# Softmax reciprocals by GpSimd partition broadcasts, projected keys transposed by the DMA crossbar, in six of eight batches

## Chip, cores, metric

One core of one Trainium2 chip (trn2). The metric is the device time of one execution in microseconds (us), median of several; lower is better. In the views PE is TensorE (PEld its weight loads), DVE is VectorE, ACT is ScalarE, POOL is GpSimd and SP is SyncE; POOLq and SPq are the DMA queues of the last two.

## The reference

Linformer attention, then a gated feed-forward stage. Per batch (8) and head (8), keys and values of 1024 positions are projected to 64 rows, then softmax over 64 columns:

```python
k_proj = np.einsum('ks,bhsd->bhkd', E, k)
v_proj = np.einsum('ks,bhsd->bhkd', F, v)
scores = (q @ k_proj^T) / sqrt(64); attn = softmax(scores)
attn_out = attn @ v_proj
x = attn_out as [8192, 512]
out = (sigmoid(x @ w_gate) * (x @ w_val)) @ w_out     # 512 -> 1536 -> 512
```

## The kernel before

Instructions are recorded in program order with what they read and write; semaphores follow from that. Each engine works through its own list in order. A "unit" is the feed-forward stage of batch b; the attention of batch b+1 is cut into ten pieces and put between its matmuls:

```python
def turn_k(ring):                      # keys transposed on TensorE
    bk = ring.next(); ob = bank[bk][:, :].bitcast(BF16)
    for r in range(NR):
        for g in range(2):
            mm(bk, ob[64*g:64*g+64, r*P:(r+1)*P], kp[:, r, :], ident[:, :], ..., tr=True, tp=(0, 64*g))
    act(kpD[...], ob[:, 0:512], [], ["kpD"], b=bk)

def den():      # ... column sums by matmul, then four reciprocals [128 x 128] into rden
def split():    # rhi = bf16(rden); rhl = both bf16 parts, for an exact-enough broadcast by matmul
def bc(rnd):    # spread the reciprocals over partitions by matmul
    for j in range(4):
        n, bk, jj = 4*rnd + j, att.next(), slice(32*j, 32*j + 32)
        mm(bk, bank[bk][:, :], bsel[jj, rnd, :, :]..., rhl[jj, :], ["bsel", "rhl"], tp=(32*j, 0))
        act(rb[:, n, :], bank[bk][:, :], [], [("rb", n)], b=bk)
def xo(r2):     # attn @ v_proj, then xT = that * rb  (VectorE; the "scaling" below)
...
return [kv, lambda: turn_k(att), lambda: sc(0), lambda: sc(1), den, split,
        lambda: bc(0), lambda: bc(1), lambda: xo(0), lambda: xo(1)]
```

`start_loads` mixes loads with iotas, from which VectorE makes the identity matrix:

```python
load_k(0)
pool(lambda e: e.iota(col_i[:, :], [[1, P]], channel_multiplier=0), w=["col_i"])
pool(lambda e: e.iota(row_i[:, :], [[1, 1]], channel_multiplier=1), w=["row_i"])
load_q_half(0, 0)
load_v(0)
# ... three more iotas, then the weights
```

The softmax here doesn't subtract the row's maximum and nothing guards it: scores larger than these inputs give would overflow.

## Time and profile before

| | us |
|---|---|
| median (lowest to highest of 4) | 581.01 (580.69 to 581.57) |
| span of the profiled run | 579.7 |
| TensorE (PE) busy | 559.1 |
| length of a repeated unit, six of them | 68.75 |

The prediction below shows the lines for these.

### The profile page before, as it was taken

The numbers are of one execution on the slowest core, as the hardware profiler recorded it, in microseconds if no ns is written. First come the engines' busy times: TensorE is split into PE (matmuls) and PEld (weight loads), VectorE is DVE, ScalarE is ACT, GpSimd is POOL, SyncE is SP. The second block draws the span as 40 slices with busy tenths as digits, with TensorE's granted clock in tenths as the row PEclk, the third lists the DMA queues.
The fourth block names the chain that finished last, engine by engine and source line by source line (L and its number), as shares of the span: only waits on it lengthen the run. The fifth ranks groups of instructions, "written<-read, shape, count | busy, mean of one in ns | idle before, by whom it ended". The sixth has DMA issues, their size and how long they took to land.

```text
span 579.7 us, 7813 instructions
## 1 busy us (share of the span) xinstructions
PE 559.1 (96%) x3150; PEld 253.9 (44%) x3206; DVE 253.3 (44%) x393; ACT 201.0 (35%) x371; POOL 30.3 (5%) x43
## 2 busy tenths in 40 slices
PE   5799899999999999999999999999999999999997
PEld 4444334444454444444444444444445444444443
DVE  2355265345633636236442365434463363633332
ACT  1454541444233351343323433243423335222220
POOL 8100010100100000000100001000000000000000
PEclk9999999999999999999999999999999999999999
DMA  9999998963943049511586027650411001000012
GB/s 153 201 206 193 139 165 155 183 133 75 162 97 75 31 109 181 91 38 48 101 162 110 19 73 117 139 92 36 74 54 38 35 21 37 37 36 20 36 37 90
DMA packets 70756, 55.04 MB, mean 95 GB/s; under 512 B 31168, under 2 KB 62400, under 8 KB 70720
## 3 DMA queue, kind: packets, MB, share of 16 engines
q0 software_dynamic: 31776, 29.89, 33.5%
q1 hardware_dynamic: 38944, 24.65, 16.5%
q8 instruction: 25, 0.41, 0.3%
q14 instruction: 11, 0.09, 0.1%
HBM read 60.29 MB, written 16.78 MB: 133 GB/s over the span
## 4 chain that ended last, share of the span: by engine, by line
PE 85%; DMA 10%; POOL 2%; DVE 1%; issue 1%; SPq 0%; POOLq 0%; DVEq 0%
PE pF L216 77%; PE pA L216 8%; DMA Qb<-in_q_dram 5%; DMA qT<-Qb 5%; DVE rden L685 1%; POOL wV L234 1%; POOL wG L234 1%; POOL KV L234 0%; POOL Qb L234 0%; SPq L622 0%; DVE rhl L695 0%; DVE ost L826 0%; DVE hT L799 0%; DVE rhi L693 0%; POOL pat_i L298 0%
## 5 line engine op out<-in xcount | busy, mean ns | idle before, releaser
L799 DVE SCALAR_TENSOR_TENSOR hT<-sig,pF 128x512 bf16<-128x512 f32 x192 | 131.2, 686 | 210.0 <-PE pF L216 140.0
L220 ACT ACTIVATE sig<-pF 128x512 f32<-128x512 f32 x192 | 115.3, 601 | 273.6 <-PE pF L216 266.1
L216 PE MATMUL pF<-xT,wG 128*128 128x512 bf16 x749 | 195.4, 380 | 2.2 <-issue 1.4
L216 PE MATMUL pF<-xT,wV 128*128 128x512 bf16 x748 | 195.1, 379 | 1.9 <-DVE xT L604 0.9
L216 PE MATMUL pF<-wO,hT 128*128 128x512 bf16 x704 | 163.4, 379 | 1.6 <-issue 1.1
L216 PEld LDWEIGHTS pF<-xT,wV 128*128 128x128 bf16 x768 | 75.1, 98 | 90.8 <-issue 0.6
L216 PEld LDWEIGHTS pF<-xT,wG 128*128 128x128 bf16 x768 | 71.2, 98 | 94.0 <-issue 14.5
L216 PEld LDWEIGHTS pF<-wO,hT 128*128 128x128 bf16 x720 | 68.7, 98 | 86.4 <-issue 5.8
L826 DVE TENSOR_SCALAR ost<-pF 128x512 f32<-128x512 f32 x60 | 41.5, 691 | 89.1 <-PE pF L216 89.1
L220 ACT ACTIVATE rb<-pA 128x512 f32<-128x512 f32 x62 | 32.2, 606 | 26.6 <-PE pA L216 26.6
L220 ACT ACTIVATE eT<-pA 128x512 bf16<-128x512 f32 x63 | 32.8, 603 | 11.3 <-PE pA L216 11.3
L733 DVE TENSOR_TENSOR xT<-pA,rb 128x512 bf16<-128x512 f32 x56 | 34.6, 680 | 0.0
L685 DVE RECIPROCAL rden<-pA 128x128 f32<-128x128 f32 x28 | 23.7, 908 | 0.0
L234 POOL DMA_DIRECT2D KV<-in_k_dram x8 | 7.2, 904 | 265.7 <-PE pF L216 208.6
L216 PE MATMUL pA<-KV,EFT 128*64 128x256 bf16 x240 | 14.6, 274 | 0.9 <-DMA KV<-in_k_dram 0.9
L220 ACT ACTIVATE kp<-pA 128x256 bf16<-128x256 f32 x8 | 3.1, 383 | 35.9 <-PE pA L216 35.9
L216 PEld LDWEIGHTS pA<-KV,EFT 128*64 128x64 bf16 x240 | 12.5, 110 | 4.1 <-issue 3.0
L216 PE MATMUL pA<-qT,kpD 64*64 64x512 bf16 (+1 forms) x140 | 10.6, 367 | 2.1 <-DMA qT<-Qb 1.8
L234 POOL DMA_DIRECT2D KV<-in_v_dram x8 | 7.1, 885 | 80.2 <-PE pA L216 80.2
L220 ACT ACTIVATE vpD<-pA 64x256 bf16<-64x256 f32 x28 | 10.5, 375 | 0.5
L216 PE MATMUL pA<-wO,hT 128*128 128x512 bf16 x47 | 10.5, 379 | 0.1
L216 PE MATMUL pA<-eT,vpD 64*64 64x512 bf16 (+1 forms) x136 | 10.4, 370 | 0.0
(72 smaller groups left out, 113.1 us busy)
## 6 DMA issues: line engine op xcount, KB each, us to landing
out_dram<-ost SPq DMA_DIRECT2D x64, 256.0 KB, 2.0
KV<-in_k_dram POOLq DMA_DIRECT2D x8, 1024.0 KB, 10.1
KV<-in_v_dram POOLq DMA_DIRECT2D x8, 1024.0 KB, 13.2
Qb<-in_q_dram POOLq DMA_DIRECT2D x7, 1024.0 KB, 15.0
wO<-in_moe_w_out_dram POOLq DMA_DIRECT2D x1, 1536.0 KB, 50.2
Qb<-in_q_dram POOLq DMA_DIRECT2D x2, 512.0 KB, 16.5
wG<-in_moe_w_gate_dram POOLq DMA_DIRECT2D x2, 512.0 KB, 23.8
wV<-in_moe_w_val_dram POOLq DMA_DIRECT2D x2, 512.0 KB, 25.6
```

Source lines behind the costliest of these rows:

```text
L216: return add("PE", lambda e: e.matmul(o, lhsT, rhs, **kw), r=r, x=[("bank", b)])
L220: return add("ACT", lambda e: e.activation(o, i, func, scale=scale), r=r, w=w, x=x)
L234: add("POOL", lambda e: e.dma_start(o, i), r=r, w=w, dma=sem)
L685: lambda e, cc=cc: e.reciprocal(rden[:, cc], bank[bk][:, cc]),
L733: lambda e, r=r, g=g, n=n, bk=bks[g]: e.tensor_tensor(xT[s][:, r, :, 256 * g : 256 * g + 256], bank[bk][:, :].rearrange("p (f c) -> p f c" ...
L799: lambda e: e.scalar_tensor_tensor(hT[blk % 2][:, m, :], sg[:, :], 1.0, bank[pv][:, :], ALU.add, ALU.mult,),
L826: lambda e: e.tensor_scalar(o[:, :], bank[pb][:, :], 0.5, None, op0=ALU.mult),
```

## The change

The intent is to take work off TensorE, which is busy throughout. In batches 2 to 7 the eight broadcasting matmuls give way to four small gathers (a reciprocal row to partitions 0, 32, 64, 96) and 16 GpSimd broadcasts, and the eight transposing matmuls to one crossbar transpose. Core of the diff:

```diff
+        kpd = sbuf("kpd", [P, NR, 2, DH], BF16)
+        rrow = sbuf("rrow", [P, 4, 512], FP32)
@@ kv()
-                keep_k(bk, 0)
+                if b == 1:
+                    ...as before; return
+                act(kpd[:, :, :, :], bank[bk][:, 0:256]... .to_broadcast([P, NR, 2, DH]), [], ["kpd"], b=bk)
                 keep_v([bk, bk], 256, ["ACT"] * 4)
+            def turn_kd():
+                if b == 1:
+                    turn_k(att)
+                    return
+                add("SP", lambda e: e.dma_start_transpose(kpD[...], kpd[...]), r=["kpd"], w=["kpD"], dma="kpD")
+            def gather():
+                for i in range(4):
+                    add("SP", lambda e, i=i: e.dma_start(rrow[::32, i, :], rden[i::32, :]), ...)
+            def spread(rnd):
+                for j in range(4):
+                    n = 4 * rnd + j
+                    for c, parts in ((1, P), (0, 64)):
+                        pool(lambda e, ...: e.partition_broadcast(
+                                rb[0:parts, n, :], rrow[32*j : 32*j+1, i, :], channels=parts),
+                            r=[("rrow", 2 * rnd + c)], w=[("rb", n)])
-                lambda: turn_k(att),
+                turn_kd,
-                split,
-                lambda: bc(0),
-                lambda: bc(1),
+                split if b == 1 else gather,
+                (lambda: bc(0)) if b == 1 else (lambda: spread(0)),
+                (lambda: bc(1)) if b == 1 else (lambda: spread(1)),
```

More of the change, by code (lines that the diff above doesn't have):

```diff
@@ L637, in kv @@
                 project((2 * b + 1) % 3, 1, [bk, bk], 256)
-                keep_k(bk, 0)
-                keep_v([bk, bk], 256, ["ACT"] * 4)
+                if b == 1:
+                    keep_k(bk, 0)
+                    keep_v([bk, bk], 256, ["ACT"] * 4)
+                    return
+                act(
+                    kpd[:, :, :, :],
+                    bank[bk][:, 0:256]
+                    .rearrange("p (r d) -> p r d", r=NR)
+                    .unsqueeze(2)
+                    .to_broadcast([P, NR, 2, DH]),
+                    [],
+                    ["kpd"],
+                    b=bk,
+                )
+                keep_v([bk, bk], 256, ["ACT"] * 4)
+            def turn_kd():
+                if b == 1:
+                    turn_k(att)
+                    return
+                add(
+                    "SP",
+                    lambda e: e.dma_start_transpose(
+                        kpD[:, :, :].rearrange("p (r h) c -> p r (h c)", h=2),
+                        kpd[:, :, :, :].rearrange("p r g d -> p (r g d)"),
+                    ),
+                    r=["kpd"],
+                    w=["kpD"],
+                    dma="kpD",
+                )
             def sc(r2):
@@ L713, in bc @@
                     act(rb[:, n, :], bank[bk][:, :], [], [("rb", n)], b=bk)
+            def gather():
+                for i in range(4):
+                    add(
+                        "SP",
+                        lambda e, i=i: e.dma_start(rrow[::32, i, :], rden[i::32, :]),
+                        r=[("rden", c) for c in range(4)],
+                        w=[("rrow", i)],
+                        dma=f"rrow{i}",
+                    )
+            def spread(rnd):
+                for j in range(4):
+                    n = 4 * rnd + j
+                    for c, parts in ((1, P), (0, 64)):
+                        pool(
+                            lambda e, n=n, i=2 * rnd + c, j=j, parts=parts: e.partition_broadcast(
+                                rb[0:parts, n, :], rrow[32 * j : 32 * j + 1, i, :], channels=parts
+                            ),
+                            r=[("rrow", 2 * rnd + c)],
+                            w=[("rb", n)],
+                        )
             def xo(r2):
```

## The prediction

> **What bounds the kernel now.** I read the page's totals first, then the table by stretches of time, then the order of instructions inside one batch. The page says how full each engine is:
>
> ```profile
> PE 559.1 (96%) x3150; PEld 253.9 (44%) x3206; DVE 253.3 (44%) x393; ACT 201.0 (35%) x371; POOL 30.3 (5%) x43
> ...
> PE 85%; DMA 10%; POOL 2%; DVE 1%; issue 1%; SPq 0%; POOLq 0%; DVEq 0%
> ```
>
> TensorE is busy for 96% of the span and carries 85% of the chain that ended last. The 10% of DMA in that chain lie at its start, in the first 72 us (the chain's list shows the first query load and the first query transposes there), and the change leaves that stage alone. From about 91 us on, the work repeats: a unit is the feed-forward stage of one batch, with the attention of the next batch put between its matmuls. The table of stretches, cut at the units (stretch, length, then busy time and instructions of PE, PEld, DVE, ACT, POOL, then granted clock, DMA share, GB/s):
>
> ```profile
> 91.50:160.50 69.00, 68.42 (x372) 30.34 (x377) 31.20 (x47) 24.64 (x46) 4.40 (x5) 1.00 0.74 138
> 160.50:229.20 68.70, 68.12 (x371) 30.26 (x376) 30.97 (x47) 24.64 (x46) 2.62 (x3) 1.00 0.47 93
> ...
> 435.50:504.30 68.80, 68.22 (x371) 30.25 (x376) 31.07 (x47) 24.64 (x46) 0.00 (x0) 1.00 0.08 31
> ```
>
> In each unit of 68.75 us PE lacks only 0.6 us of being busy throughout, at full clock; no other engine is half full. So the kernel goes as fast as PE's list is long, and six of the eight batches (the third to the eighth) change. What a change is worth is the PE time it takes out of a unit, unless something else makes PE wait.
>
> How long PE is held by the groups that go is not their "busy" (matmuls overlap, and a matmul of 512 columns is recorded as 0.38 us although the next one starts 0.216 us later: groups of four in a row start 0.865 us apart). It has to be read from starts. The timeline of PE in the unit that begins at 298 us (start, length, instructions):
>
> ```profile
> 311.50 1.03 PE L216 MATMUL pF<-xT,wV 128*128 128x512 bf16 x4
> 312.45 0.41 PE L216 MATMUL pA<-ident,kp 128*64 128x128 bf16 x8
> 312.80 2.76 PE L216 MATMUL pF<-wO,hT 128*128 128x512 bf16 x12
> ...
> 341.55 1.03 PE L216 MATMUL pF<-xT,wV 128*128 128x512 bf16 x4
> 342.51 0.39 PE L216 MATMUL pA<-rhl,bsel 32*128 32x512 bf16 x4
> 342.84 1.04 PE L216 MATMUL pF<-xT,wG 128*128 128x512 bf16 x4
> ...
> 346.30 2.75 PE L216 MATMUL pF<-wO,hT 128*128 128x512 bf16 x12
> 348.99 0.39 PE L216 MATMUL pA<-rhl,bsel 32*128 32x512 bf16 x4
> 349.31 1.04 PE L216 MATMUL pF<-xT,wG 128*128 128x512 bf16 x4
> ```
>
> The four broadcasting matmuls take 0.39 us together, not four times 0.38: they run beside each other on four bands of 32 rows.
>
> **What the Trainium skill says.** "TensorEngine Tiling (Array Packing)", Key Properties, says that tiles work independently and in parallel, and that changing the tiling mode drains the engine. The trace agrees with both: four matmuls in the time of one, and about 0.2 us more than one matmul per visit. "GPSIMD Engine Reference", 3.1, gives 769 ns measured for a loop over 512 elements per core; it has no row for a partition broadcast. Section 2.1 puts a first call of a freshly loaded routine at about 6 us more. This trace has no broadcast either; its only GpSimd computing is iota. "SBUF — State Buffer", Who interferes with whom, says that a VectorE instruction with at most one SBUF input, outside the two-port modes, does not contend with GpSimd. The frequent VectorE instructions here (gating, softmax scaling, output copy) each read one operand from PSUM and at most one from SBUF, so I expect no slowing; no run so far shows the two engines together. "VectorE: DVE Perf Modes", The three transpose paths, has 1309 ns for a 128x128 crossbar transpose; in this trace one issue of eight such blocks holds SP for 1.24 us and lands in a median of 3.1 us, and the trace decides.
>
> **The change, part by part.**
>
> Removed from PE per batch. Four matmuls at the usual spacing hold it for 4 x 0.216 = 0.865 us. Transposes of the keys: 312.80 - 311.50 - 0.865 = 0.435 us. First broadcast round: 342.84 - 341.55 - 0.865 = 0.425 us. Second: 349.31 - 346.30 - 12 x 0.216 = 0.415 us. Together 1.28 us, with the same spacings in the other units to 0.02 us. Six batches: 7.7 us. The sum of the matmuls' own durations (8 x 0.385 + 8 x 0.22 = 4.8 us a batch) would promise 29 us, and that is the trap of this profile: it would be nearly 5%.
>
> Removed elsewhere: ScalarE loses eight copies of 0.606 us and one of 0.596 us, and its copy of the keys grows from 0.38 to an estimated 0.6 us (512 columns where 256 were); VectorE loses 0.43 + 0.75 us. These lie beside PE, which waited for neither, so they are worth nothing.
>
> Added, off PE, with a deadline for each:
>
> Keys. ScalarE finishes the copy at about 308.0 in the unit above, SP issues one transpose of 128 KB (half of a query transpose), and the scores want it at 320.2 (320.67 less 0.44). That is 12 us of room. A query transpose lands in 3.1 us; the slowest of all 28, in the middle of the weight loads, took 12.2 us for twice the bytes. Here one load of V is in flight (issued at 306.9). I put it at 3 to 6 us. It meets the deadline.
>
> Reciprocals. The next three views show the room around the same place one unit earlier: VectorE, then SP's queue, then GpSimd's.
>
> ```profile
> 266.11 3.39 DVE L685 RECIPROCAL rden<-pA 128x128 f32<-128x128 f32 x4
> ...
> 286.63 2.47 DVE L733 TENSOR_TENSOR xT<-pA,rb 128x512 bf16<-128x512 f32 x4
> ...
> 293.33 2.48 DVE L733 TENSOR_TENSOR xT<-pA,rb 128x512 bf16<-128x512 f32 x4
> ```
>
> ```profile
> 273.42 9.71 SPq L622 DMA_TRANSPOSE qT<-Qb  x4
> ```
>
> ```profile
> 285.67 0.87 POOL L234 DMA_DIRECT2D KV<-in_k_dram  x1 [46.41 <-PE pF L216]
> 286.53 0.88 POOL L234 DMA_DIRECT2D Qb<-in_q_dram  x1
> 306.94 0.88 POOL L234 DMA_DIRECT2D KV<-in_v_dram  x1 [19.53 <-PE pA L216]
> ```
>
> Reciprocals end at 269.5. SP has about 4 us free before its query transposes; four gathers of 8 KB at the 0.33 us of a plain issue take it to 270.9, and at the 2.0 us to landing of the output stores the last is there by about 273; the first pair, which is what the first broadcast needs, by about 272.2. The SBUF-to-SBUF landing time is a guess from those stores.
>
> GpSimd then does 16 broadcasts of 512 elements, one after the other, and the second of each pair waits for the first by a semaphore. The iotas of this trace give 153 ns for one element and 253 or 382 ns for 128, thus 0.8 to 1.8 ns an element: as an estimate 0.56 to 1.07 us for 512. With the skill's 0.77 us in the middle and some 0.1 us for the handover I take 0.9 us each, 14.4 us in all, to 286.6. Scaling of the first half needs eight of them (279.4) and comes at 286.63 - 0.85 = 285.8; that of the second needs all (286.6) and comes at 292.5. Room: 6 us on each. A broadcast could take 1.27 us before the second deadline is touched, and about 1.4 us before PE notices through its four feed-forward banks.
>
> GpSimd's loads: K and Q of a later batch stand behind the broadcasts in its program and were issued at 285.7, when the last query transpose had landed. They move to about 287, and their data are wanted a unit later. No cost. The routine's loading stands before the first broadcasts, where GpSimd has over 20 us of nothing to do.
>
> Sum: 580.94 - 7.7 + 0 = 573.3 us.
>
> **The rivals.** First, broadcasts too slow. If one took 2 us, 16 would end at 304; VectorE, which works in order, would stand still at the scaling for about 11.5 us, the gating behind it too, and PE would lose some 9.5 us a batch: 573 + 57 = 630 us. For it: this duration is nowhere in the trace[...]. Against it: it would have to be twice my estimate. Second, the keys' transpose comes late behind the load of V or behind other work of SP. If it lost 3 us past its deadline in each batch, the time would be 591 us. Against it: 12 us of room, and SP's issue order has only stores of finished outputs ahead of it. Third, GpSimd's traffic slows VectorE or delays the loads. VectorE has 45% of each unit to spare at 31 of 68.75 us, so even gating made 20% slower leaves PE the bound; under 2 us in all. Fourth, more gain than counted: if the banks and copies set free also took out PE's 0.6 us of other gaps per unit, 3.6 us more, 569.7 us. Against it: those gaps stand at the projections and where the scaling's slot begins, and no freed wait is named there.
>
> **Range and chances.** The gain is bounded from above by what PE is freed of, so the range is short below and longer above: 572.2 to 578.5 us; the upper end allows 0.9 us of new waits a batch. The gain expected is 1.3%, so a win of over 2% would need the fourth rival in full: 1%. A loss of over 2% (above 592.6 us) needs over 3.2 us of waits a batch beyond the gain, thus broadcasts of 1.6 us or more: 7%. Within 2%: 92%.
>
> **What would show it.** Right: units of about 67.5 us instead of 68.75, PE still busy all but 0.6 us of each; no wait of VectorE's scaling for GpSimd; broadcasts starting about 0.9 us apart, done some 17 us after the reciprocals; the keys' transpose landing within 6 us. Wrong: units longer than 68.75 us, waits of the scaling on GpSimd's broadcasts or of the scores on the transpose, and PE gaps behind them. Broadcast starts over 1.4 us apart would overturn the prediction.

## More of the kernel before

Timeline of POOL, kernel before (start us, length us, engine, line, instruction, and in brackets the idle time just before and what ended it):

```profile
1.25 1.01 POOL L234 DMA_DIRECT2D KV<-in_k_dram  x1 [0.80 <-POOLq L940]
2.35 0.25 POOL L293 IOTA col_i<- 128x128 int32 x1
2.54 0.15 POOL L294 IOTA row_i<- 128x1 int32 x1
2.62 0.90 POOL L234 DMA_DIRECT2D Qb<-in_q_dram  x1
```

The first iota follows the load at once, at 2.35 us.

## The result, and the profile after

| | before | after |
|---|---|---|
| median us (lowest to highest, 4 runs each) | 581.01 (580.69 to 581.57) | 581.22 (579.88 to 581.82) |
| span of the profiled run | 579.7 | 578.0 |
| unit | 68.75 | 67.43 |
| PE busy | 559.1 | 555.5 |
| GpSimd busy | 30.3 | 101.5 |

Ratio 0.9999, 95% interval 0.9978 to 1.002: the same. The profiled run of the changed kernel was its fastest, which is why the two spans differ by more than the medians.

The puzzle is in the third row. The units did what was predicted. The table by stretches, cut at the units, changed kernel (same columns as in the prediction):

```profile
172.74:240.17 67.43, 67.43 (x362) 30.00 (x364) 29.86 (x44) 20.32 (x37) 14.43 (x19) 1.00 0.54 97
240.17:307.61 67.44, 67.44 (x363) 30.01 (x364) 29.86 (x44) 20.32 (x37) 14.43 (x19) 1.00 0.53 97
```

PE is busy throughout at full clock in 67.43 us. Six units save 6 x (68.75 - 67.43) = 7.9 us. Inside a unit everything met its deadline: timeline of POOL, then of VectorE, one batch of the changed kernel:

```profile
274.99 0.79 POOL L760 PARTITION_BROADCAST rb<-rrow  x1 [32.17 <-DMA rrow<-rden]
275.95 6.09 POOL L760 PARTITION_BROADCAST rb<-rrow  x8 [0.16 <-POOL rb L760]
282.20 5.43 POOL L760 PARTITION_BROADCAST rb<-rrow  x7 [0.16 <-POOL rb L760]
```

```profile
269.28 3.39 DVE L715 RECIPROCAL rden<-pA 128x128 f32<-128x128 f32 x4
...
288.87 2.48 DVE L785 TENSOR_TENSOR xT<-pA,rb 128x512 bf16<-128x512 f32 x4
...
295.57 2.48 DVE L785 TENSOR_TENSOR xT<-pA,rb 128x512 bf16<-128x512 f32 x4
```

The reciprocals end at 272.7, the first broadcast starts 2.3 us later, and the 16 are done at 287.6, ahead of even the first scaling at 288.9. VectorE's scaling waits for none of them.

So 7.9 us were won and, by the medians, about 8 us were lost outside the units. Following the repeated pieces backward in both traces, the projections of the third batch start at 99.1 us before and at 105.3 us after, and no part of the change has run by then. The loss is at the start: 6.2 us in these two traces, which with the 7.9 us won gives the 1.7 us between their spans. The other runs of the changed kernel were 0.8 to 1.9 us slower than the profiled one, at full clock; their traces were not kept, so where they lost that is not shown. Timeline of POOL, changed kernel:

```profile
1.24 1.01 POOL L236 DMA_DIRECT2D KV<-in_k_dram  x1 [0.80 <-POOLq L992]
13.96 0.23 POOL L295 IOTA col_i<- 128x128 int32 x1 [11.71 <-issue]
14.16 0.12 POOL L296 IOTA row_i<- 128x1 int32 x1
14.24 1.07 POOL L236 DMA_DIRECT2D Qb<-in_q_dram  x1
```

The same instructions as in the kernel before, but the first iota starts at 13.96 instead of 2.35 us, and the 11.7 us ahead of it are put down to "issue": the engine waited for nothing that the profile shows. The list of waits carries that on to TensorE:

```profile
PE pA L218 <- DVE half L331: 15.5, 1, 15.5
DVE col_f L319 <- POOL col_i L295: 14.2, 1, 14.2
POOL col_i L295 <- issue: 11.7, 1, 11.7
```

TensorE's first matmul needs the identity from VectorE, which needs the iota: PE starts at 15.5 instead of 5.6 us. The loads of Q, V and the weights stand behind the iotas and slide as well. In both compiled programs GpSimd's list has, right ahead of the first iota, an instruction that loads set 0 of its routines; the changed one has another, for set 1, ahead of the first broadcast. The one at the start costs next to nothing in the kernel before: its first iota starts 0.1 us after the load's instruction ends.

### The profile page after: what moved, and what is told of

It is laid out like the page before. It is cut to its first block, busy times and chain, and to the rows that moved or that the text cites. A ratio compares the mean times of both kernels' runs of the same rounds, so it can differ in the third digit from the quotient of the medians.

```text
span 578.0 us, 7834 instructions
## 1 busy us (share of the span) xinstructions
PE 555.5 (96%) x3110; PEld 252.1 (44%) x3110; DVE 246.4 (43%) x381; ACT 175.1 (30%) x317; POOL 101.5 (18%) x139
## 4 chain that ended last, share of the span: by engine, by line
PE 94%; issue 2%; DVE 2%; ACT 1%; POOL 0%; POOLq 0%; DVEq 0%
PE pF L218 85%; PE pA L218 9%; DVE rden L715 1%; ACT eT L222 0%; DVE xT L606 0%; ACT qT L222 0%; POOL KV L236 0%; DVE rden L553 0%; DVE vpD L464 0%; DVE identf L323 0%; DVE rhl L725 0%; DVE ost L878 0%; DVE hT L851 0%; DVE rhi L723 0%; ACT kp L222 0%
## 5 line engine op out<-in xcount | busy, mean ns | idle before, releaser
L218 PE MATMUL pF<-xT,wG 128*128 128x512 bf16 x768 | 198.6, 380 | 0.6 <-ACT rb L222 0.3
L218 PE MATMUL pF<-xT,wV 128*128 128x512 bf16 x768 | 198.2, 379 | 0.2 <-DVE xT L606 0.2
L218 PE MATMUL pF<-wO,hT 128*128 128x512 bf16 x720 | 165.4, 380 | 0.0
L760 POOL PARTITION_BROADCAST rb<-rrow x96 | 70.8, 798 | 219.3 <-DMA rrow<-rden 213.9
L218 PE MATMUL pA<-identf,EF 128*128 128x128 f32 x8 | 1.9, 421 | 15.5 <-DVE half L331 15.5
L222 ACT ACTIVATE kpd<-pA 128x512 bf16<-128x512 f32 x6 | 3.6, 597 | 28.4 <-PE pA L218 28.4
## 6 DMA issues: line engine op xcount, KB each, us to landing
Qb<-in_q_dram POOLq DMA_DIRECT2D x2, 512.0 KB, 10.3
```

The costliest lines, as they stand in the source:

```text
L218: return add("PE", lambda e: e.matmul(o, lhsT, rhs, **kw), r=r, x=[("bank", b)])
L222: return add("ACT", lambda e: e.activation(o, i, func, scale=scale), r=r, w=w, x=x)
L760: lambda e, n=n, i=2 * rnd + c, j=j, parts=parts: e.partition_broadcast(rb[0:parts, n, :], rrow[32 * j : 32 * j + 1, i, :], channels=parts),
```

## The experiments

**Theory A**: what an execution leaves in GpSimd's cores is there when the next one starts. The changed kernel ends with the broadcast's set in them, so each execution has to fetch the iota's set again before its first iota. **Rival B**: any program with two sets pays for the first load, whatever was left. **Rival C**: the start is slow for another reason, such as moved tiles or the order of transfers.

### end_iota: the changed kernel, with the first set brought back at the end

```diff
+        end_i = sbuf("end_i", [P, 8], I32)
...
+        pool(lambda e: e.iota(end_i[:, :], [[1, 8]], channel_multiplier=0), w=["end_i"])
         last = 2 * B - 1
```

> The changed kernel plus one iota of 8 columns at the end of GpSimd's program, into a tile nobody reads; the compiled program puts a load of the first routine set ahead of it. Theory A (left behind: the kernel ends with the broadcast's set in GpSimd's cores, so the next execution has to fetch the first set again before its first iota, which took 11.7 us at the start): the fetch moves to the end, where GpSimd is idle for some 80 us, the first iota starts at about 2.4 us as in the kernel before, units stay 67.43 us, time 580.9 - 7.9 = 573.1 us (572.5 to 574). Rival B (any program that uses two sets pays for its first load in every execution, whatever was left): the first iota still starts at about 14 us and the time stays at 581. Rival C (the start is slow for another reason, such as the added tiles or the order of DMAs): also 581.

Measured: correct, 572.57 us (572.18 to 573.89, 4 runs), ratio 0.9861 (0.9844 to 0.9877) to the kernel before at 580.83 us. The timeline of POOL:

```profile
1.24 1.20 POOL L237 DMA_DIRECT2D KV<-in_k_dram  x1 [0.80 <-POOLq L994]
2.80 0.25 POOL L296 IOTA col_i<- 128x128 int32 x1 [0.36 <-issue]
...
478.73 5.44 POOL L761 PARTITION_BROADCAST rb<-rrow  x7 [0.45 <-POOL rb L761]
490.97 0.13 POOL L975 IOTA end_i<- 128x8 int32 x1 [6.80 <-issue]
```

The first iota is back at 2.8 us, and an "issue" gap of 6.8 us stands ahead of the added iota, where it costs nothing. B falls: the program still uses two sets. C has no ground left: nothing at the start was edited, and `keys_only` below keeps all the added tiles and starts fast. This version beats both kernels; one instruction of 0.13 us is worth 581.22 - 572.57 = 8.65 us by medians of different rounds, 8.0 us by the two ratios to the kernel before.

### before_end_bcast: the kernel before, with the broadcast's set left behind

```diff
+        pool(lambda e: e.partition_broadcast(end_f[:, :], identf[0:1, 0:8], channels=P),
+            r=["identf"], w=["end_f"])
         last = 2 * B - 1
```

> The kernel before plus one partition broadcast of 8 columns at the end of GpSimd's program, into a tile nobody reads. Nothing else differs, and no broadcast is on any path. Theory A: the first iota starts at about 14 us instead of 2.35 us, units stay 68.75 us, time 581 + 6 to 8 = 587 to 589 us. Rival B: the same slow start, 587 to 589 (this run tells A and B together from C). Rival C: 581 us, start unchanged.

Measured: correct, 588.23 us (586.03 to 588.43, 5 runs), ratio 1.0115 (1.0096 to 1.0134). Timeline of POOL:

```profile
14.34 0.23 POOL L294 IOTA col_i<- 128x128 int32 x1 [11.90 <-issue]
...
394.04 0.28 POOL L924 PARTITION_BROADCAST end_f<-identf  x1 [10.64 <-DVE hT L800]
```

The loss is reproduced without any of the change: a tiny broadcast at the end of GpSimd's list delays the start of the (next) execution by 12 us and its end by 7.4 us. The end moves less than the iota, in part because the kernel before waited for its first transfers in that stage anyway: its PE waited 5.6 us for E and F, then 0.9, 0.7 and 0.6 us for K, Q and V. The delay shrinks from 12.0 us at the iota to 10.3 at PE's first matmul and 6.8 at the projections of the third batch.

### keys_only and recip_only: each half of the change alone

`keys_only` keeps the crossbar transpose and goes back to `split`, `bc(0)`, `bc(1)`. `recip_only` keeps gathers and broadcasts, goes back to `keep_k` and `turn_k`, and has the iota at the end.

> Of the change only the keys' transposes by the crossbar, reciprocals as before; no broadcast, so one routine set. All theories: start as before (first iota at 2.35 us); six times 0.435 us off PE: 578.3 us, units 68.3 us. If the transposes (9.4 us to landing in the changed kernel) made PE wait, it would be over 579.

Measured: correct, 578.11 us (6 runs), ratio 0.9957 (0.9941 to 0.9972); first iota at 2.35 us.

> Of the change only the reciprocals by broadcasts, keys transposed on PE as before, with the iota at the end of GpSimd's program. Theory A: fast start, six times 0.84 to 0.88 us off PE: 575.8 us (575.3 to 576.5), units 67.87 us. Rivals B and C: 583.5 to 584.

Measured: correct, 575.73 us (6 runs), ratio 0.9917 (0.99 to 0.9934); first iota at 2.80 us. Against 580.83 us the halves give 2.7 and 5.1 us, together 7.8, beside 8.3 for both (end_iota). Per batch 0.45 and 0.85 us, where the prediction had 0.435 and 0.84.

### iota_first: the fetch with less traffic beside it

The changed kernel with the first two iotas ahead of `load_k(0)`.

> The changed kernel with the first two iotas moved ahead of the first load of K, so that the fetch of the first routine set starts at about 0.4 us with no big load beside it. In the changed kernel it took 11.7 us beside a 1 MB load of K, at the end of the repaired kernel (end_iota) 6.8 us beside little. If the fetch is slowed by the load beside it: 7 to 8 us here, first iota at about 8 us, K lands at about 19 us instead of 11.7, PE's first projection at about 19.5 us instead of 21.2: 579 to 580 us. If the fetch at the start of an execution takes 11.7 us of itself: first iota at 12 us, K lands at 23 us, time 582 to 584 us.

Measured: correct, 580.35 us (579.82 to 581.35, 5 runs), ratio 0.9983 (0.9969 to 0.9998), a little over the 579 to 580 expected. The gap is neither 7 nor 12 us:

```profile
9.37 0.23 POOL L294 IOTA col_i<- 128x128 int32 x1 [8.94 <-issue]
```

The gap is 6.8 us beside one output store of 256 KB (end_iota), 8.9 us beside the loads of E and F (0.5 MB), 11.7 us when the 1 MB load of K goes out first. That fits a fetch that shares the way of the transfers, but three points at three places of the program do not settle it. Nor is the end of the list one point: the same gap is 6.7 us in `recip_only`, 7.25 in `seven` and 7.7 in `twice`, each beside one such store, so it varies by 1 us at the same traffic.

Moving the iota barely helped. The loads start late (PE waited 2.3 us for K), but the clock is a second suspect: from 20.3 to 30.5 us the granted clock was half in this profile, and the mean clock of all five runs was 0.991 to 0.997, where the changed kernel's four had 1.0. PE's first projection came 1.0 us earlier than in the changed kernel's trace, the third batch's 1.5 us later. What the move alone is worth is therefore not shown.

### seven: the second batch changed too

The repaired kernel without the exceptions for `b == 1`; that batch's attention stands in a tighter place, in the first unit.

> The repaired kernel (end_iota) with the second batch changed too, whose attention is packed into the first unit. PE's list is 1.3 us shorter, but there the scaling follows the reciprocals by 7 and 10 us, while four gathers and 16 broadcasts take 2.4 + 12.6 us and the set has to be fetched first. If the deadlines of the prediction are the right way to read this: scaling of the second half 5 to 8 us late, PE waits behind VectorE for 4 to 6 us: 575 to 578 us, worse than end_iota. If broadcasts can hide anywhere: 571.5 us.

Measured: correct, 582.85 us (582.03 to 583.85, 6 runs), ratio 1.0031; 10 us over end_iota, and worse than the 575 to 578 expected. The waits (total us, times, longest), and the timeline of PE:

```profile
PEld pA L219 <- DVE xT L779: 5.6, 4, 1.4
PEld pA L219 <- DMA kpD<-kpd: 4.7, 1, 4.7
PE pA L219 <- DVE xT L779: 4.3, 4, 1.2
```

```profile
69.96 0.73 PE L219 MATMUL pA<-qT,kpD 64*64 64x512 bf16 x8 [4.16 <-DMA kpD<-kpd]
70.62 4.30 PE L219 MATMUL pF<-wO,hT 128*128 128x512 bf16 x11
```

The late broadcasts were expected. Two things were not. The keys' transpose was late too: TensorE stood still for 4.2 us. The timeline of SP shows why:

```profile
54.94 12.37 SPq L625 DMA_TRANSPOSE qT<-Qb  x3
67.42 1.20 SPq L656 DMA_TRANSPOSE kpD<-kpd  x1
```

ScalarE had the copy ready at 59.5 us, but SP had three query transposes ahead of this one and issued it 8 us later; it then landed in 2.5 us. And after that gap the next matmuls were slow: 11 recorded in 4.30 us, where 12 take 2.75 us at full clock; the granted clock was 0.59 and 0.56 from 70 to 74 us (more under the next run). With this, leaving that batch out of the change is right.

### twice: every broadcast issued twice

```diff
-                    for c, parts in ((1, P), (0, 64)):
+                    for c, parts in ((1, P), (1, P), (0, 64), (0, 64)):
```

> The repaired kernel (end_iota) with every broadcast issued twice: 32 a batch, some 25 us. The deadline reading says: the first half's 16 are done about 1 us before their scaling, the last two rows of the second half 1 to 4 us after it, VectorE is held for about 2.6 us a batch and PE for 1 to 2.5 us: 573 + 6 to 15 = 579 to 588 us. If GpSimd's time is free altogether: 573 us.

Measured: correct, 595.11 us (593.67 to 596.05, 4 runs), ratio 1.0238 (1.022 to 1.0255). Slower, as the deadline reading says, but past its 588. Timeline of VectorE, and the table by stretches around one batch's scaling (PE granted clock is the third number from the end):

```profile
297.93 0.69 DVE L786 TENSOR_TENSOR xT<-pA,rb 128x512 bf16<-128x512 f32 x1 [1.72 <-POOL rb L761]
301.26 0.69 DVE L786 TENSOR_TENSOR xT<-pA,rb 128x512 bf16<-128x512 f32 x1 [2.64 <-POOL rb L761]
```

```profile
298.00:300.00 2.00, 1.85 (x9) 0.64 (x7) 0.62 (x1) 0.00 (x0) 1.82 (x3) 1.00 0.00 0
300.00:302.00 2.00, 0.00 (x0) 0.00 (x0) 0.74 (x2) 0.00 (x0) 1.91 (x4) 1.00 0.00 0
302.00:304.00 2.00, 1.99 (x7) 0.81 (x8) 1.35 (x3) 0.60 (x1) 0.86 (x1) 0.68 0.43 40
304.00:306.00 2.00, 1.78 (x5) 0.67 (x5) 0.48 (x1) 0.51 (x1) 0.00 (x0) 0.50 1.11 151
```

PE waits 2.2 us for the late reciprocals, and soon after it resumes the granted clock falls to half for about 3.4 us: the unit takes 71.5 instead of 67.43 us. The two parts can be told apart, as the first changed unit has the same wait (2.3 us) and no fall of the clock: it takes 69.9 us. So the lateness costs 2.5 us and the clock another 1.6 us. The Trainium skill describes such a clock on "TensorE: Matmul & The Clock Gate", Part 1: it is halved after an idle window of about 3.4 us and comes back after about 3.4 us of sustained work. The trace agrees on the way back: half clock from 302.7 to 306.1 us. It does not agree on the trigger, and the measurement decides: PE stood still for only 2.2 us here, and of the six waits of 2.1 to 2.3 us in this run four were followed by half clock and two were not. What tells them apart is not shown. My expectation had no term for it.

## Why the prediction was wrong, step by step

It said 573.3 us, range 572.2 to 578.5; measured 581.22.

- **PE time taken out: right.** 1.28 us a batch was said, 1.32 measured; start-to-start spacing, not busy time, was the right reading.
- **Broadcasts: right, a little pessimistic.** 0.9 us each was said; they start 0.78 us apart, and the 16 took 12.6 us, not 14.4. The first rival (too slow) falls for this kernel; `twice` shows that the deadline is real.
- **Gathers: right.** First broadcast 2.3 us after the reciprocals where 2.7 was said.
- **Keys' transpose: time too small, conclusion right.** 3 to 6 us was said; the median to landing is 9.4 us. Of the 12 us of room that left 2.8 us. The smallest of the six, 2.4 us with no load beside it, and the 9.4 us beside the load of V fit the worry named there. The second rival, SP's other work ahead of it, came true only in `seven`.
- **No slowing of VectorE by GpSimd: right.** Gating takes 686 ns before and 685 ns after, scaling 680 and 681. (A slip in the third rival: 31 of 68.75 us is 45% busy, so 55% to spare; its conclusion stands.)
- **The step that failed** is the pair of sentences that the change "leaves that stage alone", of the start, and that "the routine's loading stands before the first broadcasts, where GpSimd has over 20 us of nothing to do". The second is true of set 1: the first broadcast of all came 2.5 us after SP began the gathers, against 2.3 us in a later unit. But I asked what the new set costs on the way in, and not what its presence does to the load of set 0 at the start. The program carried that load all along; it cost nothing only because set 0 had been left in place. The missing term is 6 to 9 us: 6.2 in the changed kernel's trace, 7.4 by `before_end_bcast`, 8.0 or 8.65 by the repair. With the load of the first set moved to the end the predicted time is met: 572.57 us.
- **The rivals missed it.** All four looked inside a unit. "The time outside the six units" was never a line of the sum.

What stays open: what lengthens the fetch from 6.8 to 11.7 us, as told under `iota_first`. No trace shows the fetch itself: in the first 14 us of the changed kernel's the only transfers are those of E, F and K, so that the gap is a fetch is read from the load instruction in the compiled program and from what moves the gap. That the state carries over between executions is inferred from `end_iota` and `before_end_bcast`, which change nothing but the set in place at the end; no run recorded two executions in a row.

## What to carry to other kernels

A kernel's time in a repeated measurement can include what its last execution left behind: before adding the first use of a loadable GpSimd routine, ask which set is in place at the end and put a cheap instruction of the start's set behind the last use, where GpSimd is idle. When units shrink as planned and the total does not, compare the times at which the same piece starts in both traces; the first place where they differ, here the 12 us of "issue" ahead of the first iota, holds the loss. And when TensorE has no slack, a missed deadline can cost more than the gap: in `twice` the clock fell after four of the six gaps.

## What the Trainium skill lacked or had wrong

- "GPSIMD Engine Reference", 2.1, puts a freshly loaded routine's first call at about 6 us more. It does not say that the set left by one execution is what the next starts with. Here a return to the first set cost 6.7 to 7.7 us at the end (four runs), 8.9 to 11.9 us at the start (three), and 0.1 to 0.4 us where it was still in place.
- The same page has no row for a partition broadcast: 0.80 us recorded, 0.78 us from start to start, for one row of 512 fp32 values, with half of them spread to 128 and half to 64 partitions.
- "VectorE: DVE Perf Modes", The three transpose paths, has one figure, 1309 ns for 128x128. Four such blocks in one transfer from SBUF to SBUF landed in 2.4 us with no load beside it, and in 9.4 us (median) beside a 1 MB load.
- "TensorE: Matmul & The Clock Gate", Part 1, halves the clock after an idle window of about 3.4 us. In `twice` waits of 2.2 us were enough four times, as told there. In the profile of `end_iota`, the slowest of its four runs, the clock was half from 17.1 to 23.9 us, and since 5.5 us no wait of PE's had been over 0.7 us.
